# The second mixture-of-experts layer: the order of its products on TensorE, written as a chain in the source

## The chip, the core and the metric

The kernel runs on one core of a Trainium2 chip. The metric is the device time of one execution in microseconds. Times of before are the median of three runs. Engines are named as the profile names them: PE is TensorE's matmul, PEld its weight load, DVE is VectorE, ACT ScalarE, POOL GpSimd, and SP issues the DMAs.

## What is computed

```python
x = attention(q, k, v, p)              # 4 batches, 8 heads, 576 rows -> 2304 x 512
h = x @ w_in                           # first MoE: 512 -> 2048 -> 512
x = (h * clip(h + 3, 0, 6) / 6) @ w_out
P = exp(x @ w_gate - max)              # 2304 x 8, then 8 rounds of row and column norms
out = zeros
for e in range(8):                     # second MoE: 512 -> 1024 -> 512, per expert
    out += P[:, e:e+1] * (maximum(x @ w1[e], 0) @ w2[e])
```

All is float32. A float32 product is made on PE of three products of halves: a high half that is rounded (`fp32r`) and the remainder, so that each 128x128 weight tile costs three matmuls (high by high, high by low, low by high).

## The kernel before

**Tiling.** The 2304 rows are 6 blocks of 384 columns (`TB`). The 8 experts of the second MoE are cut into 32 groups of 256 hidden units. Blocks are taken in three pairs, called passes here. Stage A (to about 440 us) is attention and the first MoE. Stage B (about 440 to 1010 us) is the first pass, blocks 0 and 1, over all 32 groups. Stage C (about 1010 to 2061 us) is the other two passes; in each of them two groups make a unit, so it has 16 units.

**First layer** (`layer1b`, lines 1137 to 1185). For a pair of blocks and one group it makes seven products instead of eight (a Strassen scheme of the Winograd kind): operands `a11, s3, s2, a22, s1, a12, s4` of the blocks against sums of weights in `wa` and `wb`. A product is six matmuls of 384 columns into a PSUM bank (tag `ph`, four banks). Three of the seven add onto a bank that holds an earlier product, so the earlier value must have been read out: `held` copies it (ACT, line 385), `plus` adds it (DVE, line 1165). Four results leave through `finish`: in stage B a Relu on ACT and a split into halves `hs`; in stage C one DVE operation that also multiplies by the share of the expert (line 1128).

**Second layer.** In stage B `layer2b` makes, per group, six products of six matmuls with 512 columns, lines 1463 to 1465, each added into the result by DVE (line 1487). In stage C `layer2s` makes 14 products of six matmuls with 384 columns per unit (lines 1373 to 1375), seven operands by two halves `c`, into four banks of tag `po`; `summed` (DVE, line 1385) adds each into the result. Its operands are made by `h_operands` from the eight results of the unit's two first layers: 14 splits (ACT, line 1321, then a subtraction on POOL or DVE, line 1328) and 8 sums, `mix` (line 1334). `a11` and `s3` can be made after the first of the two first layers, the other five only after the second.

**Weights.** In stage B `combined`, `plain_second` and `keep_second` load, combine and split each group's weights (DVE, POOL and ACT) and store the results in DRAM. Stage C only loads them back (`w` 1024 KB, `w1x` 768 KB, `w2s` 512 KB each) through SP, into two, two and seven buffers.

**What sets the order.** Nothing is issued in the order of the source. `Order.op` records operations with their dependences; `Order.run` builds the order of every engine's queue before the kernel runs: it takes, again and again, the open operation that can start first by the planner's own clock, ties by `prio`. Its clock goes by costs such as `t_pe`, `t_dve`, `t_pool`; `SYNC` (0.2 us) lies between an operation and whoever depends on it. An operation of `alt` may go to POOL or DVE, whichever ends first, with `spare` added to DVE's side; `copy` likewise to ACT or DVE. Each engine then executes its queue in that order. Before the change the products of stages B and C have no order of their own, only operands, banks and `prio`.

## Time and profile before

| | us |
|---|---|
| median of three runs (2077.38 to 2078.06) | 2077.91 |
| the profiled execution, its own time | 2076.28 |
| its span, first to last instruction | 2074.5 |
| PE busy | 1921.8 (93%) |
| DVE busy | 1559.1 (75%) |
| POOL busy | 999.7 (48%) |
| ACT busy | 873.1 (42%) |

Busy shares are means over three stages. A busy PE is not a PE at its peak: its matmuls overlap, so the distance from one start to the next counts, not the duration. The clock column of a window is the share of TensorE's full clock that was granted; 1.00 is 2.4 GHz and 0.5 is 1.2 GHz.

### The profile page before, as it was taken

The page shows a single profiled execution, that of the slowest core. Times are in us where ns is not written, and L with a number is a line of the kernel's source. Part 1 is how long each engine was busy: PE and PEld are TensorE (multiplying, and loading weights), DVE is VectorE, ACT ScalarE, POOL GpSimd, SP SyncE. Part 2 cuts the span into 40 slices and gives each one's busy share as a digit, 9 for nine tenths or more (in the row PEclk, how much of TensorE's full clock was granted, in tenths as well). Part 3 has the DMA queues.
Part 4 walks back from the last instruction along what each step waited for, and adds up shares of the span by engine and source line. Part 5 has one row for each costly group of instructions (what it writes and reads, how often), then busy time and mean ns, then how long its engine had stood idle before and what let it go on. Part 6 is the DMA issues. An engine that isn't in the chain of part 4 may idle for free.

```text
span 2074.5 us, 31172 instructions
## 1 busy us (share of the span) xinstructions
PE 1921.8 (93%) x11199; PEld 1800.5 (87%) x11199; DVE 1559.1 (75%) x2536; ACT 873.1 (42%) x1898; POOL 999.7 (48%) x886
## 2 busy tenths in 40 slices
PE   6999999998899999898999999999989999999997
PEld 4889999897788878887898988989889898988987
DVE  6765674559988887888668778787787878778786
ACT  5764663345455555555432323223243323323232
POOL 3333562357667665667434435344364434334343
PEclk8999999999999999999999999999999999999998
DMA  9931230027788777777777677777777767777762
GB/s 200 198 77 42 62 117 20 3 80 270 269 289 292 277 279 249 279 269 260 265 252 237 228 230 238 235 238 228 230 224 242 239 218 238 232 240 237 220 223 71
DMA packets 189563, 430.22 MB, mean 207 GB/s; under 512 B 52304, under 2 KB 102624, under 8 KB 177120
## 3 DMA queue, kind: packets, MB, share of 16 engines
q1 hardware_dynamic: 189408, 428.23, 64.0%
q8 instruction: 88, 1.44, 0.3%
q14 instruction: 67, 0.55, 0.1%
HBM read 305.94 MB, written 122.23 MB: 206 GB/s over the span
## 4 chain that ended last, share of the span: by engine, by line
PE 57%; DVE 28%; issue 7%; DMA 3%; ACT 3%; POOL 2%; SPq 1%; DVEq 0%; ACTq 0%; POOLq 0%
PE ph L1151 7%; PE ph L1153 7%; PE ph L1152 7%; DVE tmp L1334 7%; PE po L1373 5%; PE po L1374 5%; PE po L1375 5%; DVE tmp L1165 3%; DVE tmp L1128 3%; PE po L1028 3%; PE po L1030 3%; PE po L1029 3%; PE po L1465 2%; PE po L1463 2%; PE po L1464 2%
## 5 line engine op out<-in xcount | busy, mean ns | idle before, releaser
L1328 POOL TENSOR_TENSOR xy<-tmp,xy 128x384 fp32r<-128x384 f32 x191 | 234.3, 1246 | 307.9 <-PE ph L1153 233.1
L1328 POOL TENSOR_TENSOR ax<-tmp,ax 128x384 fp32r<-128x384 f32 x154 | 187.5, 1234 | 282.3 <-PE ph L1153 221.5
L385 ACT ACTIVATE tmp<-ph 128x384 f32<-128x384 f32 x282 | 137.6, 488 | 440.8 <-PE ph L1153 434.9
L503 POOL TENSOR_TENSOR hs<-tmp,hs 128x384 fp32r<-128x384 f32 x193 | 211.0, 1103 | 231.9 <-ACT hs L498 224.7
L1165 DVE TENSOR_TENSOR tmp<-ph,tmp 128x384 f32<-128x384 f32 x288 | 157.4, 552 | 116.2 <-PE ph L1153 100.3
L1334 DVE TENSOR_TENSOR tmp<-tmp,tmp 128x384 f32<-128x384 f32 x253 | 226.7, 914 | 6.3 <-POOL ax L1328 0.5
L1385 DVE TENSOR_TENSOR acc<-po,acc 128x384 f32<-128x384 f32 x304 | 160.8, 552 | 84.8 <-PE po L1375 84.5
L1373 PE MATMUL po<-xy,w2s 128*128 128x384 f32 x492 | 172.8, 351 | 34.0 <-ACT ax L1321 15.3
L1321 ACT ACTIVATE xy<-tmp 128x384 fp32r<-128x384 f32 x246 | 126.8, 524 | 140.6 <-DVE tmp L1334 87.0
L1373 PE MATMUL po<-ax,w2s 128*128 128x384 f32 x404 | 144.0, 356 | 31.7 <-ACT xy L1321 17.2
L1374 PE MATMUL po<-xy,w2s 128*128 128x384 f32 x492 | 170.9, 347 | 0.7 <-DVE xy L1328 0.7
L1375 PE MATMUL po<-xy,w2s 128*128 128x384 f32 x492 | 168.9, 343 | 0.0
L1321 ACT ACTIVATE ax<-tmp 128x384 fp32r<-128x384 f32 x202 | 104.1, 523 | 126.0 <-DVE tmp L1334 71.3
L1151 PE MATMUL ph<-ax,w 128*128 128x384 f32 x448 | 152.9, 341 | 3.5 <-ACT tmp L385 2.0
L1463 PE MATMUL po<-w,hs 128*128 128x512 f32 x384 | 150.8, 393 | 4.0 <-DVE acc L1487 2.7
L1487 DVE SCALAR_TENSOR_TENSOR acc<-po,Pr,acc 128x512 f32<-128x512 f32 x168 | 123.2, 743 | 40.8 <-PE po L1465 40.4
L1153 PE MATMUL ph<-ax,w 128*128 128x384 f32 x448 | 152.4, 340 | 0.0
L1152 PE MATMUL ph<-ax,w 128*128 128x384 f32 x448 | 152.2, 340 | 0.0
L1465 PE MATMUL po<-w,hs 128*128 128x512 f32 x384 | 149.8, 390 | 0.5 <-DVE hs L503 0.5
L1464 PE MATMUL po<-w,hs 128*128 128x512 f32 x384 | 149.7, 390 | 0.0
L1374 PE MATMUL po<-ax,w2s 128*128 128x384 f32 x404 | 142.3, 352 | 0.5 <-POOL ax L1328 0.5
L1128 DVE SCALAR_TENSOR_TENSOR tmp<-tmp,PB 128x384 f32<-128x384 f32 x192 | 133.8, 699 | 10.5 <-DMA PB<-pd 5.5
(230 smaller groups left out, 5579.5 us busy)
## 6 DMA issues: line engine op xcount, KB each, us to landing
w2s<-w2d SPq DMA_DIRECT2D x224, 512.0 KB, 4.3
w<-w1d SPq DMA_DIRECT2D x64, 1024.0 KB, 6.0
w1x<-w1d SPq DMA_DIRECT2D x64, 768.0 KB, 4.7
raw<-in_moe_w_dram SPq DMA_DIRECT2D x64, 512.0 KB, 5.2
w1d<-w SPq DMA_DIRECT2D x32, 1024.0 KB, 5.0
w1d<-w1x SPq DMA_DIRECT2D x32, 768.0 KB, 5.1
w2d<-w SPq DMA_DIRECT2D x96, 256.0 KB, 3.6
w2d<-H SPq DMA_DIRECT2D x64, 256.0 KB, 4.0
```

Source lines behind the costliest of these rows:

```text
L503: lambda e: e.tensor_tensor(dst(w.t[1]), src(), as_f32(dst(w.t[0])), ALU.subtract),
L1128: lambda: nc.vector.scalar_tensor_tensor(c.t, src(), 0.0, pb.t[:, half * TB:(half + 1) * TB], ALU.max, ALU.mult),
L1151: nc.tensor.matmul(out, wh[:, at + c, :], bh[:, c, :], start=first and c == 0, **on)
L1152: nc.tensor.matmul(out, wh[:, at + c, :], bl[:, c, :], start=False, **on)
L1153: nc.tensor.matmul(out, wl[:, at + c, :], bh[:, c, :], start=False, **on)
L1165: t_dve(n), lambda: nc.vector.tensor_tensor(u.t, ps.t[:, :n], u.t, ALU.add),
L1321: t_act(TB), lambda: nc.scalar.activation(dst(0), t.t, AF.Copy),
L1328: lambda e: e.tensor_tensor(dst(1), t.t, as_f32(dst(0)), ALU.subtract),
L1334: t_dve(TB), t_pool(TB), lambda e: e.tensor_tensor(dst.t, i0.t, i1.t, how),
L1373: nc.tensor.matmul(o, wh[:, f, cs], ah[:, f, :], start=begin and f == 0, **on)
L1374: nc.tensor.matmul(o, wh[:, f, cs], al[:, f, :], start=False, **on)
L1375: nc.tensor.matmul(o, wl[:, f, cs], ah[:, f, :], start=False, **on)
```

## The change

`next_pe` puts every product of `layer1b`, `layer2b` and `layer2s` into one chain: each depends on the one before it, with no `SYNC` between them (`tight`). The three functions become generators that stop after each product, and `by_turns` steps through the first layer of the next group, taking one product of the waiting second layer after each of its own. In stage C a unit's two first layers, 14 products, so alternate with the 14 second-layer products of the unit before. At the border of the two passes of stage C seven second-layer products go ahead and seven take turns; after the last unit all 14 go alone.

The planner's costs are set anew for the operations around these products: 0.174 and 0.228 us a matmul, 0.56 us for a DVE operation from PSUM, 0.8 (DVE) and 1.2 (POOL) for one on two SBUF operands; `mix` now goes to DVE only where it ends 0.5 us sooner. `fourth_phase` opens its buffers when the weights are prepared; four `w2s` buffers and three operand buffers open later (`fifth_phase`), when the last second layer of stage B is done; the output of a pass (`written`) is recorded after the first unit's first layers of the next.

```diff
+PITCH, WIDE = 0.174, 0.228
+MIXES = 0.5
+D_PSUM, D_BOTH, D_SHARE, A_PSUM, A_SBUF, P_BOTH = 0.56, 0.8, 0.72, 0.5, 0.53, 1.2
...
-                a.ready = max(a.ready, o.end + SYNC)
+                a.ready = max(a.ready, o.end + (0.0 if a.tight and o.tight else SYNC))
...
         for tag, n, count, first in (("PB", 2 * TB, 2, 0), ("U", 2 * TB, 1, 0), ("tmp", TB, 6, 6)):
             places(tag, fixed(later, tag, n, count, first))
             opened(tag, count)
+
+    def fifth_phase():
+
         wide = [wp.tile([128, 2048], F32R, tag=f"w2_{i}", name=f"w2s{i}") for i in range(2)]
-        places("w2s", [t[:, i:i + 1024] for t in wide for i in (0, 1024)] + [*spot["raw"][:2], (dp, "ms0")])
-        opened("w2s", 7)
+        places("w2s", [t[:, i:i + 1024] for t in wide for i in (0, 1024)])
+        opened("w2s", 4)
         places("xy", spot["hs"])
         opened("xy", 3)
+
+    def raw_over():
+
+        places("w2s", [*spot["raw"][:2], (dp, "ms0")])
+        opened("w2s", 3)
...
+    def next_pe(cost, fn, **kw):
+
+        turns["b"] = [pe(cost, fn, after=turns["b"], tight=True, **kw)]
...
-                t_dve(TB),
+                D_SHARE,
...
-            pe(t_pe(n, 6), mm, reads=[w, src], writes=[ps], after=turns["l1"], **kw)
+            next_pe(6 * PITCH, mm, reads=[w, src], writes=[ps], **kw)
 
         def held(ps):
 
             u = tmp()
-            copy(lambda: u.t, lambda: ps.t[:, :n], n, reads=[ps], writes=[u], **quick)
+            copied(lambda: u.t, lambda: ps.t[:, :n], reads=[ps], writes=[u], **quick)
...
-                t_dve(n), lambda: nc.vector.tensor_tensor(u.t, ps.t[:, :n], u.t, ALU.add),
+                D_PSUM, lambda: nc.vector.tensor_tensor(u.t, ps.t[:, :n], u.t, ALU.add),
...
         b0, b1, b2 = (psum("ph") for _ in range(3))
         product(b0, wa, 0, o["a11"], True)
         p1 = held(b0)
+        yield
         product(b1, wb, 2, o["s3"], True)
         p7 = held(b1)
+        yield
         product(b0, wb, 0, o["s2"])
         u2 = held(b0)
...
         product(b0, wa, 4, o["s4"])
         finish(tmp(), 0, 1, b0)
-        return order.all[-1]
+        yield
...
             high = act(
-                t_act(TB), lambda: nc.scalar.activation(dst(0), t.t, AF.Copy),
+                A_SBUF, lambda: nc.scalar.activation(dst(0), t.t, AF.Copy),
                 reads=[t], fills=[hop[nm]], after=begun[-1:] if c == 0 else [], **quick,
             )
             if c == 0:
                 begun.append(high)
             alt(
-                t_dve(TB), t_pool(TB),
+                D_BOTH, P_BOTH,
...
             alt(
-                t_dve(TB), t_pool(TB), lambda e: e.tensor_tensor(dst.t, i0.t, i1.t, how),
-                reads=reads, writes=[dst], **quick,
+                D_BOTH, P_BOTH, lambda e: e.tensor_tensor(dst.t, i0.t, i1.t, how),
+                reads=reads, writes=[dst], spare=MIXES, **quick,
...
-            pe(t_pe(TB, 3 * NFC), mm, reads=[w, hop[nm]], writes=[ps], **kw)
+            next_pe(6 * PITCH, mm, reads=[w, hop[nm]], writes=[ps], **kw)
...
-            if last and nm == "s2":
-                both(cb, 0)
-                both(cb, 2)
-                both(ca, 2)
+                if last and nm == "s2" and c:
+                    both(cb, 0)
+                    both(cb, 2)
+                    both(ca, 2)
+                yield
...
-            pe(t_pe(512, 3 * NFC), mm, reads=[w2, hs], writes=[ps], **kw)
+            next_pe(3 * NFC * WIDE, mm, reads=[w2, hs], writes=[ps], **kw)
...
+        waiting = iter(())
+
+        def by_turns(one, other):
+
+            for _ in one:
+                next(other, None)
+
+        done, preparing = [], []
...
                 stored[4] = [*wa.writers, *wb.writers]
                 w2, r = plain_second(g, turn)
+                preparing += order.all[at:]
...
-                done.append(layer1b(i, ops[0], wa, wb, rectified(prios(i)[1], hs)))
-                for h in (1, 0):
-                    layer2b(i, g, h, w2, hs[h])
+                by_turns(layer1b(i, ops[0], wa, wb, rectified(prios(i)[1], hs)), waiting)
+                done.append(turns["b"][0])
+                waiting = chain_of(*[layer2b(i, g, h, w2, hs[h]) for h in (1, 0)])
...
+            at = len(order.all)
             keep_second(d2, ws, rs, turn - 0.7)
-        order.op([("", 0.0, fourth_phase)], after=order.all[begun:])
-        late_ops = [o for o in order.all[begun:] if fin[0] in o.holds or fin[1] in o.holds]
+            preparing += order.all[at:]
+        order.op([("", 0.0, fourth_phase)], after=preparing)
+        order.op([("", 0.0, raw_over)], after=preparing)
...
+                if behind and d2 == 0:
+                    for _ in range(NFC * 7 // 2):
+                        next(waiting)
                 for n in range(2):
                     wa, wb = kept_first(G1 + 2 * d2 + n, turn + 0.1 + 0.1 * n)
                     one_of = {}
-                    done.append(layer1b(i, ops[pr], wa, wb, shared(prios(i)[1], pb, one_of)))
+                    by_turns(layer1b(i, ops[pr], wa, wb, shared(prios(i)[1], pb, one_of)), waiting)
...
+                            [("", 0.0, fifth_phase)],
+                            after=[o for o in order.all if any(h.tag in ("w2", "hs") for h in o.holds)],
+                        )
+                        late_ops = [o for o in order.all[begun:] if fin[0] in o.holds or fin[1] in o.holds]
+                        order.op([("", 0.0, more)], after=late_ops)
...
+                if behind and d2 == 0:
+                    written(i, pr - 1, behind)
+                    i += 1
                 w2s = {nm: kept_second(d2, nm, turn + 0.5 + 0.01 * n) for n, nm in enumerate(PLACE)}
                 turn += 1
-                layer2s(i, hop, w2s, C, U, d2 == len(doubles) - 1)
+                waiting = layer2s(i, hop, w2s, C, U, d2 == len(doubles) - 1)
                 i += 1
+            behind = C
             if pr + 1 < NB // 2:
                 ops[pr + 1] = operands(pr + 1, 45, lambda n: [turns["hop"][-1]])
-            written(i, pr, C)
-            i += 1
+        by_turns(waiting, iter(()))
+        written(i, pr, C)
```

Lines of the changed program are 27 to 34 higher: 1178 to 1180 are the first layer's matmuls, 1406 to 1408 and 1497 to 1499 the second layer's, 1361 is the split's subtraction and 1367 `mix`.

PE in stage C, before: the end of the next unit's first first-layer product, and the first product of operand `a12` (here in `xy11`), whose bank is `po_0`, and the start of the next (`c` = 1).

```order
L1153 MATMUL ph_0_13128<-xy7_10112,w10_13013 128x384
L1373 MATMUL po_0_13062<-xy11_13060,w2s1_10688 128x384
L1374 MATMUL po_0_13062<-xy11_13060,w2s1_10688 128x384
L1375 MATMUL po_0_13062<-xy11_13060,w2s1_10688 128x384
L1373 MATMUL po_0_13062<-xy11_13060,w2s1_10688 128x384
L1374 MATMUL po_0_13062<-xy11_13060,w2s1_10688 128x384
L1375 MATMUL po_0_13062<-xy11_13060,w2s1_10688 128x384
L1373 MATMUL po_1_13075<-xy11_13060,w2s1_10688 128x384
```

And with the change, the same operand's first product (here from `ax1`) in a unit of the same pass:

```order
L1180 MATMUL ph_3_13365<-ax0_112,w10_13225 128x384
L1406 MATMUL po_2_13377<-ax1_113,w2s2_13210 128x384
L1407 MATMUL po_2_13377<-ax1_113,w2s2_13210 128x384
L1408 MATMUL po_2_13377<-ax1_113,w2s2_13210 128x384
L1406 MATMUL po_2_13377<-ax1_113,w2s2_13210 128x384
L1407 MATMUL po_2_13377<-ax1_113,w2s2_13210 128x384
L1408 MATMUL po_2_13377<-ax1_113,w2s2_13210 128x384
L1178 MATMUL ph_2_13474<-ax0_112,w10_13225 128x384
```

Before, this product follows one product of the next unit and is followed by the rest of its own second layer; now it follows five products of the next unit and has one more on either side of it.

PE in stage B, before: a first-layer product into `ph_2`, one other product, and the next product onto `ph_2`.

```order
L1153 MATMUL ph_2_7806<-ax1_113,w11_7700 128x384
L1151 MATMUL ph_3_7947<-ax1_113,w11_7700 128x384
L1152 MATMUL ph_3_7947<-ax1_113,w11_7700 128x384
L1153 MATMUL ph_3_7947<-ax1_113,w11_7700 128x384
L1151 MATMUL ph_3_7947<-ax1_113,w11_7700 128x384
L1152 MATMUL ph_3_7947<-ax1_113,w11_7700 128x384
L1153 MATMUL ph_3_7947<-ax1_113,w11_7700 128x384
L1151 MATMUL ph_2_7806<-xy6_5333,w11_7700 128x384
```

And with the change, around a product of `layer2b` (1497 to 1499), where the bank `ph_1` of the last row was last written two products before the one that ends in the first row:

```order
L1180 MATMUL ph_2_7931<-ax1_113,w11_7673 128x384
L1497 MATMUL po_1_7943<-w20_7643,hs2_7814 128x512
L1498 MATMUL po_1_7943<-w20_7643,hs2_7814 128x512
L1499 MATMUL po_1_7943<-w20_7643,hs2_7814 128x512
L1497 MATMUL po_1_7943<-w20_7643,hs2_7814 128x512
L1498 MATMUL po_1_7943<-w20_7643,hs2_7814 128x512
L1499 MATMUL po_1_7943<-w20_7643,hs2_7814 128x512
L1178 MATMUL ph_1_7821<-xy6_5363,w11_7673 128x384
```

Two products of one bank had one first-layer product between them; now they have one first-layer and two second-layer products.

POOL in stage C, before, at the end of a unit's first layers: subtractions of splits only.

```order
L1328 TENSOR_TENSOR xy11_13060<-tmp9_13001,xy11_13060 128x384
L1328 TENSOR_TENSOR xy12_13072<-tmp10_13040,xy12_13072 128x384
L1328 TENSOR_TENSOR xy13_13084<-tmp7_12965,xy13_13084 128x384
L1328 TENSOR_TENSOR xy12_13072<-tmp6_13028,xy12_13072 128x384
L1328 TENSOR_TENSOR xy13_13084<-tmp0_12957,xy13_13084 128x384
L1328 TENSOR_TENSOR xy14_13097<-tmp3_12857,xy14_13097 128x384
L1328 TENSOR_TENSOR xy15_13111<-tmp9_13001,xy15_13111 128x384
```

And with the change, at the same place:

```order
L1367 TENSOR_TENSOR tmp10_12865<-tmp10_12865,tmp11_12999 128x384
L1367 TENSOR_TENSOR tmp5_12816<-tmp10_12865,tmp5_12816 128x384
L1361 TENSOR_TENSOR xy6_13047<-tmp3_12983,xy6_13047 128x384
L1367 TENSOR_TENSOR tmp6_12938<-tmp7_12841,tmp6_12938 128x384
L1361 TENSOR_TENSOR xy11_13064<-tmp7_12841,xy11_13064 128x384
L1361 TENSOR_TENSOR ax1_113<-tmp8_12964,ax1_113 128x384
L1361 TENSOR_TENSOR ax1_113<-tmp9_13077,ax1_113 128x384
```

Sums (`mix`, 1367) now stand among the subtractions. Over the whole program `mix` stands 127 times on POOL and 129 times on DVE, where it was 3 and 253; the subtractions of these splits are 319 on POOL and 129 on DVE, where they were 345 and 103. The number of matmuls and of DMAs is the same.

## Rows read from the trace of the kernel before

**Rows 1.** The page: busy time, share of the span and instructions of each engine.
```profile
PE 1921.8 (93%) x11199; PEld 1800.5 (87%) x11199; DVE 1559.1 (75%) x2536; ACT 873.1 (42%) x1898; POOL 999.7 (48%) x886
```

**Rows 2.** Windows of two stretches: busy us and instructions per engine, clock, DMA share.
```profile
core 0: us, PE busy (x) PEld busy (x) DVE busy (x) ACT busy (x) POOL busy (x), PEclk, DMA share, GB/s
600.00:1000.00 400.00, 370.15 (x1812) 330.19 (x1811) 330.25 (x427) 212.15 (x453) 259.26 (x224) 0.98 0.76 267
1100.00:2000.00 900.00, 840.03 (x4646) 818.41 (x4645) 697.94 (x1079) 277.31 (x572) 374.52 (x309) 0.98 0.72 232
```

**Rows 3.** PE timeline: start, duration, line, operation; 384 columns, then 512 columns.
```profile
1499.73 0.34 PE L1153 MATMUL ph<-xy,w1x 128*128 128x384 f32 x1
...
1511.17 0.34 PE L1153 MATMUL ph<-ax,w 128*128 128x384 f32 x1
...
705.39 0.39 PE L1463 MATMUL po<-w,hs 128*128 128x512 f32 x1
...
713.33 0.39 PE L1465 MATMUL po<-w,hs 128*128 128x512 f32 x1
```

**Rows 4.** Waits of PE, 1100 to 2000 us: total us, times, longest.
```profile
PE po L1373 <- ACT xy L1321: 25.2, 14, 2.0
PE po L1373 <- ACT ax L1321: 23.0, 12, 2.8
PE po L1373 <- DVE acc L1385: 8.3, 17, 1.2
```

**Rows 5.** PE timeline at one such wait, and the window behind it.
```profile
1162.52 0.41 PE L1373 MATMUL po<-ax,w2s 128*128 128x384 f32 x1 [1.78 <-ACT xy L1321]
...
1164.30 0.53 PE L1374 MATMUL po<-ax,w2s 128*128 128x384 f32 x1
1164.62 0.53 PE L1375 MATMUL po<-ax,w2s 128*128 128x384 f32 x1
...
1163.40:1166.80 3.40, 3.40 (x12) 3.33 (x12) 3.40 (x7) 0.53 (x1) 1.71 (x2) 0.51 0.08 29
```

**Rows 6.** DVE groups, 1100 to 2000 us: busy us, mean ns, idle before.
```profile
L1334 DVE TENSOR_TENSOR tmp<-tmp,tmp 128x384 f32<-128x384 f32 x216 | 193.4, 914 | 5.7 <-POOL ax L1328 0.5
L1385 DVE TENSOR_TENSOR acc<-po,acc 128x384 f32<-128x384 f32 x272 | 143.8, 552 | 71.9 <-PE po L1375 71.6
L1128 DVE SCALAR_TENSOR_TENSOR tmp<-tmp,PB 128x384 f32<-128x384 f32 x164 | 114.3, 697 | 4.6
L1328 DVE TENSOR_TENSOR xy<-tmp,xy 128x384 fp32r<-128x384 f32 x44 | 46.0, 1046 | 0.0
```

**Rows 7.** POOL and ACT groups of the same stretch.
```profile
L1328 POOL TENSOR_TENSOR xy<-tmp,xy 128x384 fp32r<-128x384 f32 x164 | 200.9, 1244 | 267.2 <-PE ph L1153 214.2 <-ACT xy L1321 53.0
...
L1321 ACT ACTIVATE xy<-tmp 128x384 fp32r<-128x384 f32 x208 | 107.6, 524 | 119.8 <-DVE tmp L1334 73.5 <-DVE tmp L1128 46.3
L385 ACT ACTIVATE tmp<-ph 128x384 f32<-128x384 f32 x164 | 80.2, 489 | 378.2 <-PE ph L1153 376.0
```

**Rows 8.** Single lines, whole span: shortest/median/longest ns, first and last start.
```profile
L1334 DVE TENSOR_TENSOR tmp<-tmp,tmp x253: 543/902/1386, 1022.5 to 2050.2; 128x384 f32<-128x384 f32 x127
...
L1328 POOL TENSOR_TENSOR xy<-tmp,xy x191: 997/1325/1357, 1030.2 to 2047.2; 128x384 fp32r<-128x384 f32 x191
...
L1165 DVE TENSOR_TENSOR tmp<-ph,tmp x288: 506/551/559, 452.7 to 2040.4; 128x384 f32<-128x384 f32 x144
```

**Rows 9.** Groups of PE and DVE, 600 to 1000 us, and the waits of PE.
```profile
L1463 PE MATMUL po<-w,hs 128*128 128x512 f32 x276 | 108.0, 391 | 2.7 <-DVE acc L1487 2.7
...
L1487 DVE SCALAR_TENSOR_TENSOR acc<-po,Pr,acc 128x512 f32<-128x512 f32 x139 | 102.0, 744 | 34.3 <-PE po L1465 34.1
...
PE ph L1151 <- DVE tmp L1165: 26.7, 16, 3.6
```

**Rows 10.** Two lines of 430 to 1010 us: shortest/median/longest ns.
```profile
L1248 DVE TENSOR_TENSOR T<-T,H x37: 675/1221/1812, 462.0 to 977.9; 128x512 fp32r<-128x512 f32 x37
...
L503 POOL TENSOR_TENSOR hs<-tmp,hs x193: 1000/1022/1550, 59.6 to 1002.3; 128x384 fp32r<-128x384 f32 x193
```

32 lines of the change are left out of this document (25 added, 7 removed).

## The prediction

> **What bounds the kernel now.** I read the page's first section first: PE is busy 93% of the span, DVE 75%, POOL 48% and ACT 42% [rows 1]. So the end is PE's, and the question is how far each stage of it is from PE's own pace. That pace I took from the timeline of undisturbed stretches: 67 matmuls of 384 columns start from 1499.73 to 1511.17, 66 steps of 173.3 ns; 36 matmuls of 512 columns from 705.39 to 713.33, 35 steps of 226.9 ns [rows 3]. The floor of a stage B group is then 42 x 0.1733 + 36 x 0.2269 = 15.45 us, that of a stage C unit 168 x 0.1733 = 29.12 us.
>
> Then the windows, to see how far the stages are from it. Stage B, 600 to 1000 us: line 1463 ran 276 times, 12 a group, so 23.0 groups in 400 us, **17.39 us a group** [rows 2, 9]. Stage C, 1100 to 2000: 4646 matmuls, 24 of them the output's transposes (six times four, by the source), so 4622 / 168 = 27.5 units in 900 us, **32.7 us a unit** [rows 2]. The distances are 1.94 and 3.6 us.
>
> What they consist of: PE idle is 900 - 840.0 = 60.0 us in C, 2.2 a unit, and 400 - 370.2 = 29.8 us in B, 1.3 a group [rows 2]. The waits say on whom. In C it is line 1373, the second layer's first matmul, that waits: 25.2 + 23.0 us for ACT's split of an operand (1321) and 8.3 us for DVE's sum (1385), 56.5 of the 60.0 us [rows 4]. In B it is the first layer waiting for DVE's read of a bank (1165), 26.7 of 29.8 us [rows 9]. The rest, 1.4 us a unit and 0.6 a group, is PE running slower or starting again: after a wait of 1.78 us the matmuls start 0.32 us apart for 3.4 us at a granted clock of 0.51, the lower of the two levels [rows 5]. Such stretches come back through C (mean clock 0.98 [rows 2]).
>
> **The change part by part.**
>
> Stage C, the operands' wait. Five of seven operands can only be made when both first layers are done. Before, one product of the next unit and four of the second layer stood between that point and the first product of `a12`: 5 x 1.04 = 5.2 us of cover, and PE waited about 2 us behind them. Now five products of the next unit and four of the second layer stand there (the order's first two pieces): 9.4 us, 4.2 us more than before, against waits of at most 2.8 us [rows 4]. Later operands gain more: up to twelve more first-layer products lie ahead of `s4`. So this term, 48.2 / 27.5 = 1.75 us a unit, goes. What is late next is not an operand but a bank: DVE's sum of 0.55 us [rows 6] must be done before the bank is written again, four products later before (4.2 us) and four pairs later now (8.3 us). Those 8.3 / 27.5 = 0.3 us go as well, unless DVE itself runs behind.
>
> Does it? DVE is busy 697.9 / 27.5 = 25.4 us a unit [rows 2]. By the order 124 `mix` leave it and 26 subtractions come, over 32 units: -124 x 0.914 + 26 x 1.05 = -86 us [rows 6], 2.7 a unit, so 22.7 us. At the floor of 29.12 that is 78%, as now (25.4 of 32.7). POOL is busy 13.6 us a unit and takes 124 more at 1.24 and loses 26: +122 us, 3.8 a unit, so 17.4 us, 60% [rows 2, 7]. ACT keeps 10.1 us. None of them reaches PE's floor.
>
> That DVE needs longer when POOL is busy is in the rows: 1334 takes 543 ns at the shortest, 902 in the median and 1386 at the longest, POOL's 1328 997 and 1325, while 1165, with one operand in PSUM, stays at 506 to 559 [rows 8]. With POOL at 60% instead of 42% the 14 DVE operations of a unit that read two SBUF operands (4 `mix`, 4 subtractions, 6 of 1128) lie between no change and 1.39 us each. They are in the 22.7 at 0.91, 1.05 and 0.70 [rows 6]; at 1.39 it would be 1.9 + 1.4 + 4.2 = 7.5 us more, 30.2 us. I take a third of that, 25 us (86%), nearest to the medians.
>
> The Trainium skill (SBUF — State Buffer, "Who interferes with whom") says of this that a VectorE instruction with two SBUF inputs and a GpSimd instruction that reads SBUF hold one port pair in turn, each for its whole length. The trace agrees in what it shows (543 to 1386 ns against 506 to 559). By that rule moving sums from the engine that holds the pair for 0.55 us to one that holds it for 1.0 us speaks against this change; its result is the third case below.
>
> So PE should be fed in C, but with DVE at 86% and every engine's queue in a fixed order I leave something: one wait of a sum per unit as now (8.3 / 17 = 0.49 us [rows 4]) and 0.4 us of lower clock, 0.9 in all. A unit goes from 32.7 to 30.0, a gain of 2.7 us, **86 us over 32 units**. Bounds: half of the idle and nothing of the clock (1.1 us, 35) to all but 0.4 us (3.2 us, 102).
>
> Loads in C: the DMA share is 0.72 [rows 2]; the same bytes in 30.0 us make 0.78. Stage B runs at 0.76 and 267 GB/s, more than the 232 x 32.7 / 30.0 = 253 GB/s needed. The loads are issued when a product frees a buffer, now evenly over the unit instead of in bursts. I cost them at nothing. The operand and weight buffers that open later hold nothing up: the first second layer of C starts a unit later than they did.
>
> Stage B. The bank that waits for 1165 had one first-layer product as cover, 1.04 us; now one first-layer and two second-layer products, 1.04 + 2 x 1.36 = 3.8 us (the order's next two pieces). By cover alone the 1.16 us a group would go. But DVE is busy 330.3 / 23.0 = 14.4 us a group [rows 2], 93% of the floor, and no DVE work leaves stage B to speak of. Of that, 1487 (102.0 us) and 1165 (69 x 0.551 = 38) read PSUM, 6.1 us; 8.3 us read two SBUF operands and are stretched: 1248 has a median of 1221 ns against 675 at the shortest [rows 9, 10]. At the shortest lengths these are 8.3 x 675 / 1221 = 4.6 us, and POOL's 259.3 / 23.0 = 11.3 us are 11.3 x 1000 / 1022 = 11.1 [rows 2, 10]; if one always waits for the other, as the stretch suggests, that is 15.7 us, more than PE's floor. So DVE and POOL become the bound soon after PE's waits are gone. I take 16.8 us a group (DVE at 86%, the two together at 93%), a gain of 0.6, half of the waits, over 28 of 32 groups since the first four run beside the routing: **17 us**. Bounds: 0 to 1.6 us, 45 in all.
>
> Edges. The last unit's 14 second-layer products have no partner in either program; at the border of the passes seven go ahead alone and seven first-layer products go alone later, much as before. Zero, within 5 us either way. The chain itself adds a wait only in the planner; PE's queue is in order before and after. But a late product now also holds up the other layer's product behind it, which the planner used to let past; that is the fifth case.
>
> Sum: 86 + 17 = 103 us. The profiled execution took 2076.28 (span 2074.5 and 1.8 around it), 1.6 under the median of three. The span would be 1971.5, the median **1975 us**.
>
> **The rivals.**
> 1. As above, 1975. For it: PE's waits are nearly all of the two kinds that get more cover. Against it: DVE's stretch.
> 2. Stage B gains nothing: the 15.7 us of DVE and POOL in turn, with the gaps that two queues in fixed order leave, are its 17.39 us now. 2078 - 86 = 1992. For it: DVE's stretch there; against it: PE's waits for 1165 have a cover that is too short by 1 to 3 us, which is what changes.
> 3. Stage C is paced by DVE stretched to its limit: 30.2 us of work at 97% fill makes 31.1 us a unit, a gain of 1.6 x 32 = 51; with B's 17, 2010; without, 2027.
> 4. Everything goes: C at 29.5 a unit and B at 15.8: 102 + 45 = 147, so 1931.
> 5. Slower. ACT's queue is in order: the copies of `held` (0.49 us [rows 7]) stand between splits (1321) that wait for `mix`, now half of them on POOL at 1.24 us. The bank is needed again 3.1 us after its product. If the four `mix` of a unit on POOL each come so late that a copy behind them misses that by 1.24 us, PE stands 5.0 us a unit, and no product of the other layer may pass: 29.12 + 5.0 + 1.4 (the clock as now) = 35.5 us, +2.8 x 32 = 90; with 17 from B, 2151. It decides from 3.6 us of waits a unit, 0.26 us per pair. Against it: planned 1.2 us for POOL is what the rows show, and 3.1 us of cover hides two such operations in a row.
>
> That the change doesn't do what it says is excluded by the order: the products alternate one by one in all of stages B and C.
>
> **How the numbers follow.** Chances: the first 0.52, the second 0.19, the third 0.13, the fourth 0.09, the fifth 0.05, and 0.02 for an end within 0.2%, which is what a measurement here can tell from no change (4 us). Faster by more 0.93, slower by more 0.05. The range takes in the fourth case's end and the third's: 1931 to 2027.
>
> **What would show it.** In the changed profile: no wait of a second-layer product for ACT's split in steady units, units of about 30 us between equal products of stage C, the granted clock at 1.00 in more of its slices; POOL near 58 to 60% there; `mix` and split subtractions on DVE longer than 0.91 and 1.05 us; stage B at 16.8 us a group with PE still waiting for DVE. Case 2 shows as a stage B of unchanged length with DVE above 90%; case 3 as DVE above 95% in C and PE waiting for 1385; case 5 as first-layer products waiting for ACT's copies. The forecast is wrong if PE's idle time in C stays above 1.5 us a unit, or if a load's landing ends PE's waits.

## The result: 1982 us, and the profile after

The changed kernel took **1982.03 us** in the median (1980.3 to 1984.49, four runs), the kernel before 2077.98 beside it. The ratio is 0.9536, 95% interval 0.9519 to 0.9552: faster by 4.6%. The forecast was 1975 us. The sum is right within 7 us, its parts are not: stage C gave 12.6 us more than forecast, stage B 12 less, and 8 us that were not forecast went at the end of stage A. That these nearly cancel is luck.

Both programs run the same 11199 matmuls, and both traces hold them all, so that an equal number left marks an equal point in the work. I cut both where 7600 are left (the routing is over) and where 5200 are left (early in stage C). Windows of before, then of after; the columns are start and end of the window, its length, busy us and instructions of each engine, PE's granted clock, DMA share and GB/s:

```profile
0.00:526.10 526.10, 489.79 (x3598) 443.09 (x3599) 344.20 (x756) 285.00 (x666) 240.53 (x245) 0.98 0.40 109
526.10:1052.80 526.70, 488.47 (x2401) 438.64 (x2400) 427.01 (x568) 273.65 (x584) 331.46 (x289) 0.98 0.78 272
1052.80:2074.50 1021.70, 943.56 (x5203) 918.81 (x5201) 787.87 (x1214) 314.44 (x649) 427.71 (x353) 0.97 0.70 225
```

```profile
0.00:534.30 534.30, 494.01 (x3598) 444.85 (x3599) 343.40 (x756) 287.86 (x669) 242.89 (x249) 0.97 0.39 107
534.30:1056.00 521.70, 488.41 (x2402) 439.28 (x2401) 435.15 (x557) 278.07 (x591) 334.86 (x294) 0.98 0.79 276
1056.00:1979.10 923.10, 904.51 (x5203) 900.14 (x5201) 738.92 (x1122) 302.21 (x642) 510.82 (x444) 1.00 0.72 248
```

Stage C gave 98.6 us, stage B 5.0, and the stretch ahead of it cost 8.2. The sum, 95.4, is the difference of the spans. Stage B's 5.0 us are no more than two traces of one order differ by, as e8 shows below.

Inside the stages, after (they answer to [rows 2]; in 600 to 1000 us the 1840 matmuls, 78 a group, make 16.96 us a group):

```profile
600.00:1000.00 400.00, 376.21 (x1840) 335.63 (x1839) 341.29 (x428) 218.92 (x466) 266.12 (x236) 0.98 0.80 280
1100.00:1400.00 300.00, 300.00 (x1729) 300.00 (x1728) 242.18 (x371) 96.77 (x205) 165.68 (x144) 1.00 0.75 260
```

In C, 1729 / 168 = 10.29 units in 300 us are **29.15 us a unit**, against a floor of 29.12. DVE is busy 23.5 us of it (81%), POOL 16.1 (55%). PE's waits from 1050 to 1900 us are few, and all lie at the border of the two passes, where before the same list was one wait or two in each unit [rows 4]:

```profile
PE po L1406 <- ACT acc L402: 2.7, 1, 2.7
PE ph L1179 <- DVE xy L1100: 1.6, 2, 1.4
PE ph L1178 <- ACT tmp L412: 1.4, 1, 1.4
```

Earlier, in the first unit of stage C (1000 to 1050 us), PE waits once for a load of weights from DRAM; before, the same stretch had 3.5 us of waits, for DVE and POOL:

```profile
PE ph L1178 <- DMA w<-w1d: 4.5, 1, 4.5
```

The groups of DVE and POOL in C (1100 to 1900 us, answering to [rows 6, 7]) show the stretch that the forecast feared: `mix` on DVE went from 914 to 1057 ns, the product with the share (`L1155`) from 697 to 800, while operations with one operand in PSUM stayed at 550. The splits' subtractions on DVE did not lengthen (1046 before, 1038 after). PE didn't wait for any of them.

```profile
L1418 DVE TENSOR_TENSOR acc<-po,acc 128x384 f32<-128x384 f32 x261 | 143.5, 550 | 87.3 <-PE po L1408 87.2
L1155 DVE SCALAR_TENSOR_TENSOR tmp<-tmp,PB 128x384 f32<-128x384 f32 x161 | 128.6, 800 | 4.5
L1367 DVE TENSOR_TENSOR tmp<-tmp,tmp 128x384 f32<-128x384 f32 x109 | 113.2, 1057 | 0.9
L1367 POOL TENSOR_TENSOR tmp<-tmp,tmp 128x384 f32<-128x384 f32 x107 | 110.3, 1031 | 293.1 <-DVE tmp L1155 291.0
L1361 DVE TENSOR_TENSOR xy<-tmp,xy 128x384 fp32r<-128x384 f32 x74 | 75.9, 1038 | 1.3
```

Stage B keeps its kind of wait (600 to 950 us, answering to the last line of [rows 9]); the first line is of before, the second of after:

```profile
PE ph L1151 <- DVE tmp L1165: 23.1, 15, 3.1
PE ph L1178 <- DVE tmp L1192: 19.2, 11, 2.5
```

And what the forecast didn't have: at the end of stage A, PE's timeline shows first-layer products of stage B from 394.6 us on, where they had begun at 439.1, and gaps around them. Here are three of the rows, then two windows of after, then the same two of before:

```profile
394.55 0.45 PE L1178 MATMUL ph<-ax,w 128*128 128x384 f32 x1 [0.36 <-DVE tmp L1035]
...
397.12 0.44 PE L1178 MATMUL ph<-ax,w1x 128*128 128x384 f32 x1 [1.26 <-DVE tmp L1035]
...
410.41 1.40 PE L1557 MATMUL ph<-acc,wg 128*32 128x384 f32 x5 [2.54 <-DVE pwl L979]
```

```profile
400.00:425.00 25.00, 22.11 (x155) 19.55 (x154) 7.76 (x16) 6.01 (x13) 5.32 (x6) 0.93 0.00 1
425.00:450.00 25.00, 23.18 (x145) 20.65 (x143) 9.36 (x18) 10.76 (x24) 9.00 (x10) 1.00 0.08 32
```

```profile
400.00:425.00 25.00, 25.00 (x168) 23.36 (x167) 9.67 (x20) 6.07 (x12) 4.38 (x6) 1.00 0.01 1
425.00:450.00 25.00, 25.00 (x149) 24.08 (x148) 12.28 (x20) 9.10 (x20) 9.37 (x9) 1.00 0.00 1
```

The old code put a first-layer product behind `turns["l1"]`, the last first-layer product of stage A; `next_pe` dropped that dependence, so that the planner let stage B's first products in between stage A's last ones.

### The profile page after: what moved, and what is told of

Read it like the earlier page. It is cut to its first block, busy times and chain, and to the rows that moved or that the text cites. A ratio compares the mean times of both kernels' runs of the same rounds, so it can differ in the third digit from the quotient of the medians.

```text
span 1979.1 us, 30944 instructions
## 1 busy us (share of the span) xinstructions
PE 1886.9 (95%) x11199; PEld 1784.3 (90%) x11199; DVE 1517.5 (77%) x2434; ACT 868.1 (44%) x1901; POOL 1088.6 (55%) x985
## 4 chain that ended last, share of the span: by engine, by line
PE 71%; DVE 12%; DMA 6%; POOL 4%; issue 3%; ACT 3%; SPq 1%; POOLq 0%; DVEq 0%; ACTq 0%
PE ph L1178 9%; PE ph L1180 9%; PE ph L1179 9%; PE po L1408 8%; PE po L1407 8%; PE po L1406 8%; PE po L1055 3%; PE po L1057 3%; PE po L1056 3%; DMA raw<-in_moe_w_dram 2%; PE ph L1017 2%; PE po L1499 2%; PE po L1497 2%; PE po L1498 1%; PE ph L1019 1%
## 5 line engine op out<-in xcount | busy, mean ns | idle before, releaser
L1367 POOL TENSOR_TENSOR tmp<-tmp,tmp 128x384 f32<-128x384 f32 x127 | 131.2, 1033 | 347.3 <-DVE tmp L1155 344.9
L1354 ACT ACTIVATE xy<-tmp 128x384 fp32r<-128x384 f32 x296 | 147.2, 519 | 344.1 <-DVE tmp L1155 299.6
L1361 POOL TENSOR_TENSOR xy<-tmp,xy 128x384 fp32r<-128x384 f32 x209 | 252.8, 1223 | 45.4 <-ACT xy L1354 44.3
L1406 PE MATMUL po<-xy,w2s 128*128 128x384 f32 x592 | 198.9, 336 | 1.3 <-DVE U L1418 1.3
L1408 PE MATMUL po<-xy,w2s 128*128 128x384 f32 x592 | 199.6, 337 | 0.0
L1407 PE MATMUL po<-xy,w2s 128*128 128x384 f32 x592 | 199.6, 337 | 0.0
L1178 PE MATMUL ph<-ax,w 128*128 128x384 f32 x512 | 174.0, 340 | 3.2 <-ACT tmp L412 2.0
L1179 PE MATMUL ph<-ax,w 128*128 128x384 f32 x512 | 173.4, 339 | 0.6 <-POOL ax L1100 0.6
L1180 PE MATMUL ph<-ax,w 128*128 128x384 f32 x512 | 173.5, 339 | 0.0
L1155 DVE SCALAR_TENSOR_TENSOR tmp<-tmp,PB 128x384 f32<-128x384 f32 x192 | 153.3, 799 | 5.3
L1361 POOL TENSOR_TENSOR ax<-tmp,ax 128x384 fp32r<-128x384 f32 x110 | 134.6, 1236 | 21.2 <-ACT ax L1354 20.6
L1354 ACT ACTIVATE ax<-tmp 128x384 fp32r<-128x384 f32 x152 | 76.7, 519 | 144.3 <-DVE tmp L1155 118.9
L1367 DVE TENSOR_TENSOR tmp<-tmp,tmp 128x384 f32<-128x384 f32 x129 | 132.1, 1042 | 1.1
L525 ACT ACTIVATE hs<-tmp 128x384 fp32r<-128x384 f32 x224 | 117.2, 523 | 23.4 <-DVE tmp L1035 11.8
```

The costliest lines, as they stand in the source:

```text
L1178: nc.tensor.matmul(out, wh[:, at + c, :], bh[:, c, :], start=first and c == 0, **on)
L1179: nc.tensor.matmul(out, wh[:, at + c, :], bl[:, c, :], start=False, **on)
L1180: nc.tensor.matmul(out, wl[:, at + c, :], bh[:, c, :], start=False, **on)
L1354: A_SBUF, lambda: nc.scalar.activation(dst(0), t.t, AF.Copy),
L1361: lambda e: e.tensor_tensor(dst(1), t.t, as_f32(dst(0)), ALU.subtract),
L1367: D_BOTH, P_BOTH, lambda e: e.tensor_tensor(dst.t, i0.t, i1.t, how),
```

## The experiments

Each kernel's trace holds the 11199 matmuls and is cut in the same way, in us: from the first instruction to the matmul with 7600 left (A), from there to the one with 5200 left (B), and on to the start of the last matmul (C). B ends with some 200 matmuls of stage C. Each ratio is to executions of the kernel before that ran beside that kernel. The cuts are of one execution each: the beginning of A, down to 10500 matmuls left, took 95.9 to 100.9 us in five kernels with one order of PE there (changed, e1, e2, e3, e12).

| kernel | median | ratio (95%) | A | B | C |
|---|---|---|---|---|---|
| before | 2077.98 | 1 | 526.3 | 526.7 | 1012.0 |
| changed | 1982.03 | 0.9536 (0.9519 to 0.9552) | 534.6 | 521.6 | 913.6 |
| e1 chain from stage A | 1974.53 | 0.9502 (0.9476 to 0.9528) | 529.0 | 521.6 | 913.6 |
| e2 stage B in blocks | 2016.22 | 0.9690 (0.9656 to 0.9723) | 539.0 | 554.5 | 913.6 |
| e12 blocks turned | 1988.05 | 0.9554 (0.9541 to 0.9567) | 529.9 | 534.3 | 913.6 |
| e3 stage C in sevens | 1992.22 | 0.9589 (0.9555 to 0.9623) | 533.1 | 526.7 | 917.8 |
| e5 chain, old elementwise costs | 1987.5 | 0.9579 (0.9563 to 0.9596) | 534.2 | 525.3 | 916.0 |
| e4 all costs, no chain | 2012.2 | 0.9679 (0.9650 to 0.9708) | 525.0 | 527.8 | 949.3 |
| e10 elementwise costs, no chain | 1994.85 | 0.9610 (0.9578 to 0.9642) | 521.4 | 524.9 | 928.8 |
| e9 matmul costs, no chain | 2153.32 | 1.0368 (1.0339 to 1.0397) | 530.7 | 514.6 | 1097.2 |
| e8 spare for `mix`, no chain | 2076.85 | 1.0006 (0.9994 to 1.0018) | 528.4 | 521.4 | 1013.0 |
| e6 no low halves of sums in B | 1961.86 | 0.9455 (0.9437 to 0.9473) | 531.5 | 506.6 | 913.5 |
| e7 preparation on POOL | 1971.36 | 0.9490 (0.9472 to 0.9508) | 525.4 | 521.7 | 913.7 |
| e11 chain in C only | 1967.98 | 0.9478 (0.9461 to 0.9496) | 527.5 | 511.5 | 913.5 |

### The end of stage A (e1)

```diff
+        turns["b"] = turns["l1"]
 
         def by_turns(one, other):
```

> The changed kernel with one line more: the chain begins behind stage A's last first-layer product, the dependence that every first-layer product of the second MoE had before. Theory: the changed kernel lost 9 us ahead of stage B because two of its products, with their operands and copies, went into stage A's tail (the last second-layer product of stage A starts at 459.5 us instead of 450.2, the routing's first matmul at 467.8 instead of 456.2). Then stage A's last product comes back to 450 to 452 us, and the total falls by 7 to 11 us, from 1982 to 1971 to 1975. Rival: the time before stage B is hidden by DVE's routing chain and the weights of stage B, which set its pace anyway; then stage A ends earlier but the total stays within 2 us of 1982.

The chain begins behind stage A's last first-layer product, and the stretch A falls from 534.6 to 529.0 us, the median by 7.5. PE is busy again in the two windows that had gaps:

```profile
400.00:425.00 25.00, 25.00 (x170) 23.36 (x169) 9.14 (x21) 6.91 (x14) 5.01 (x5) 1.00 0.01 1
425.00:450.00 25.00, 24.71 (x145) 23.48 (x144) 11.85 (x18) 9.00 (x20) 8.50 (x8) 1.00 0.00 1
```

So 5.6 of the 8.3 us lost ahead of stage B come from the dropped dependence. Where stage A ends, between 8600 and 7800 matmuls left, the three kernels are clearer apart: 129.6 us before, 137.9 with the change, 130.7 in e1. B and C don't move, and the expected 7 to 11 us came (the two intervals just overlap).

### Stage C: the chain or the costs (e3, e4, e5, e8, e9, e10)

Is it the one-by-one order? e3 keeps the chain and lets seven products of each layer alternate:

```diff
-                    by_turns(layer1b(...), waiting)
+                    by_turns(layer1b(...), iter(()))
+                    for _ in range(NFC * 7 // 2):
+                        next(waiting, None)
```

> The changed kernel, but in stage C seven first-layer products alternate with seven second-layer products of the unit before, not one with one; chain, look-ahead and costs stay. Theory one (stage C's gain is the cover of the operands, which a look-ahead of a unit gives in any grain): waits for ACT's split stay away, a unit takes 29.1 to 29.5 us, total 1982 to 1995. Theory two (the fine grain itself is needed, since banks and the two engines' queues get bursts): a unit takes 30.5 us or more, total 2025 or above.

C takes 4.2 us more, 29.35 us a unit, so the grain matters little; what counts is that other products stand between the end of a unit's first layers and the second-layer product that would wait (how many is counted below). (Another 5.1 us lie ahead of the cut: PE's order is the changed kernel's down to 5455 matmuls left, and the loss comes behind that point, where stage C begins, 58.5 instead of 53.8 us to 5200 left.)

e4 takes the costs of the change and no chain: the kernel before with `PITCH`, `WIDE`, `MIXES`, `D_*`, `A_*` and `P_BOTH` in the same places.

> The kernel before with the planner's new costs alone: the costs of these products, of DVE from PSUM, of DVE and POOL on two SBUF operands, and the 0.5 us for sums; no chain, no turns. Theory one (the order does it): stage C stays near 32 us a unit with waits for ACT's split, total 2060 to 2085. Theory two (true costs and sums on POOL do it): stage C falls to 29.1 to 30 us a unit, total 1980 to 2005.

Neither theory had this: 62.7 of stage C's 98.4 us come with the planner's costs alone. The window and the waits of e4:

```profile
1100.00:1400.00 300.00, 292.11 (x1669) 288.99 (x1668) 250.16 (x371) 90.04 (x190) 161.94 (x134) 1.00 0.76 250
```

```profile
PE po L1386 <- DVE U L1398: 18.8, 13, 4.1
PE po L1386 <- DVE acc L1398: 5.9, 7, 0.9
```

30.2 us a unit, and the wait that is left is for DVE's sum of a bank, not for a split. e5 asks the reverse, the chain with the old elementwise costs, which send `mix` back to DVE:

```diff
-MIXES = 0.5
-D_PSUM, D_BOTH, D_SHARE, A_PSUM, A_SBUF, P_BOTH = 0.56, 0.8, 0.72, 0.5, 0.53, 1.2
+MIXES = 0.0
+D_PSUM, D_BOTH, D_SHARE, A_PSUM, A_SBUF, P_BOTH = 0.465, 0.465, 0.465, 0.37, 0.415, 0.976
```

> The changed kernel with its chain of products, but with the elementwise costs of before in the planner (0.465 us for each DVE operation of 384 columns, 0.37 and 0.415 for ACT, 0.976 for POOL, nothing added to DVE's side for mix): mix goes back to DVE (254 of 256). Theory one, the chain gives the operands their cover whatever the planner believes of the other engines: stage C keeps 29.2 to 29.6 us a unit, and the time is 1980 to 1995 us. Theory two, the chain fixes only PE's order and the balance of DVE and POOL needs the new costs: DVE at 25 us a unit runs behind, stage C goes to 30 us a unit or more, and the time is 2005 us or more.

Its window of stage C, and the group of `mix` on DVE (1100 to 1900 us):

```profile
1100.00:1400.00 300.00, 300.00 (x1728) 300.00 (x1728) 240.38 (x405) 97.60 (x205) 135.49 (x112) 1.00 0.75 258
```

```profile
L1367 DVE TENSOR_TENSOR tmp<-tmp,tmp 128x384 f32<-128x384 f32 x214 | 174.7, 816 | 1.0
```

C is 2.4 us longer than with the new costs, at 29.17 us in steady units, with POOL busy 135 us of 300 instead of 166 and DVE nearly the same: with the chain, the elementwise costs and the balance of DVE and POOL hardly count. (e5 keeps the new matmul costs and the change's other edits, when buffers open and where the output is recorded; these were not taken out one by one.) e8, the kernel before with `spare=0.5` on `mix`, was to test that balance without a chain.

> The kernel before with one number changed: mix goes to DVE only where it ends 0.5 us sooner than on POOL. No chain, and all other costs of the planner as before. Theory one, the part of the gain that came with the costs alone (2012 us) comes from the balance of DVE and POOL in stage C: the time falls to 2045 us or less. Theory two, it comes from the order of the products that the planner chooses with truer durations, and that order is nearly the old one here: 2060 to 2085 us.

It tests less than it should: with DVE's old cost of 0.465 us the margin moves one `mix` (252 on DVE, 253 before). Time and C are those of before. But it shows how far two traces of one order differ: up to 1000 us, all of stage B but its end, every engine runs the same operations in the same order as before, and B took 521.4 us against 526.7. So a gain of 5 us in B is not shown by one trace. e9 and e10 cut the costs of e4 in two: e9 has this edit and those of the two second layers' matmuls (`PITCH`, `WIDE`), e10 the others (`D_*`, `A_*`, `P_BOTH`, `MIXES`).

```diff
-            pe(t_pe(n, 6), mm, reads=[w, src], writes=[ps], after=turns["l1"], **kw)
+            pe(6 * PITCH, mm, reads=[w, src], writes=[ps], after=turns["l1"], **kw)
```

> The kernel before with only the planner's costs of the elementwise operations set anew (DVE 0.56, 0.72 and 0.8 us, ACT 0.5 and 0.53, POOL 1.2, and 0.5 us on DVE's side for mix), no chain, matmul costs as before; mix goes to POOL 95 times of 256 instead of 3, and second-layer products come between first-layer ones more often (runs of 1 to 4, as with all costs). Theory one, the gain of the run with all new costs came from the matmul costs: 2060 us or more, stage C 32 us a unit or more. Theory two, it came from the elementwise costs, because a planner that sees the operands come later puts first-layer products in front of the product that would wait: stage C 31 us a unit or less and 2035 us or less.

> The kernel before with only the planner's costs of a matmul set anew (0.174 and 0.228 us instead of 0.163 and 0.216), no chain and all elementwise costs as before; mix stays on DVE (254 of 256). In the run with all new costs and no chain (2012 us) stage C took 30.3 us a unit and its products alternated more. Theory one, that gain came from the matmul costs, by which the planner's PE order follows the real one: stage C 31 us a unit or less and 2035 us or less. Theory two, it came from the elementwise costs: stage C 32 us a unit or more, 2060 to 2085 us.

e10 went as its theory two says (29.5 us a unit in 1100 to 1400 us), e9 came out slower than either theory allowed. The halves pull in opposite directions: the elementwise costs alone bring 83.2 of the 98.4 us, the matmul costs alone, 0.011 to 0.012 us more for each, lose 85.2. The order of PE's products of one unit (1 a first layer, 2 the second layer), from the traces in steady units; e10 has two kinds of unit in turn. In the rows of before, e9 and e10 the first run of 1 and the next single 1 are still this unit's own first layers, and only later ones the next unit's; in the last two rows all are the next unit's:

```
before   111111111111 22 1 22 1 2222222222
e9       111111111111 2 1 222 1 2222222222
e10      111111111 222 1 2 11111 2222222222
         11111111 2 1 222 11 2 11 222222222
changed  1212121212121212121212121212
e3       1111111 2222222 1111111 2222222
```

A planner that sees the elementwise operations end later keeps three or four more first-layer products for the place where PE would wait, as the chain does everywhere. e9's order on PE differs from that of before by one product, and its units took 300 x 168 / 1453 = 34.7 us. So the trace must say what PE waits for. PE at one unit of e9 (start, duration), then DVE and ACT at that time:

```profile
1512.88 0.34 PE L1154 MATMUL ph<-xy,w 128*128 128x384 f32 x1
1516.53 0.66 PE L1374 MATMUL po<-ax,w2s 128*128 128x384 f32 x1 [3.31 <-ACT tmp L386]
```

```profile
1512.88 1.81 DVE L1335 TENSOR_TENSOR tmp<-tmp,tmp 128x384 f32<-128x384 f32 x2
1514.61 1.34 DVE L1329 TENSOR_TENSOR ax<-tmp,ax 128x384 fp32r<-128x384 f32 x1
1515.88 0.55 DVE L1386 TENSOR_TENSOR U<-po,U 128x384 f32<-128x384 f32 x1
...
1515.15 0.47 ACT L386 ACTIVATE tmp<-ph 128x384 f32<-128x384 f32 x1
```

The row names ACT's copy, which ended at 1515.62, 0.9 us before PE started. DVE's sum ended at 1516.43, 0.10 us before, and does so at 21 of the 22 waits of over 1.5 us at this line from 1100 to 1900 us. The product is the first of operand `a12`: it adds onto the bank that `a11`'s product filled, and so waits for the sum that reads that bank, besides its operand. The sum stands in DVE's queue behind two `mix` and a subtraction. In the kernel before the same product waits for both too:

```profile
1128.67 1.19 DVE L1334 TENSOR_TENSOR tmp<-tmp,tmp 128x384 f32<-128x384 f32 x1
1129.78 0.55 DVE L1385 TENSOR_TENSOR U<-po,U 128x384 f32<-128x384 f32 x1
...
1129.89 0.52 ACT L1321 ACTIVATE xy<-tmp 128x384 fp32r<-128x384 f32 x1 [0.59 <-DVE tmp L1334]
...
1130.43 0.41 PE L1373 MATMUL po<-xy,w2s 128*128 128x384 f32 x1 [1.75 <-ACT xy L1321]
```

The sum ends 0.10 us ahead of PE there, the split 0.01 us. But this split is not one of `a12`: ACT stood idle ahead of it until the `mix` that ends at 1129.86, so it splits that result, while `a12` is split from a first-layer result as it stands, without a `mix`. A row names the operation that ended last on an engine that the product waits for, whether the product needs that operation or not. At all 26 waits of [rows 4] that name a split it is so: the split follows a `mix` by 0.03 or 0.04 us and ends 0.01 us before PE, and the sum of `a11`'s bank, behind that same `mix` in DVE's queue, ends 0.10 us before. So the 48.2 us are waits for the sum, in the kernel before as in e9 and, mostly one product later, in e4. What removes them is room ahead of the product. Between a unit's last first-layer product and its first product of `a12` stand 3 products before (PE waits 1.8 us), 4 in e9 (3.3 us, behind the longer queue above), 5 or 6 in e4 and e10, 10 with the change and 18 in e3; from 5 on PE no longer waits at this product in steady units. Between the two products of the bank stand 5 before and only 3 in e3, so what counts is the time that DVE has for the `mix` ahead of the sum, not the distance within the bank.

### Stage B (e2, e6, e7, e11, e12)

e2 keeps the chain and makes stage B's order blocks of seven first-layer and six second-layer products:

```diff
-                by_turns(layer1b(...), waiting)
+                by_turns(layer1b(...), iter(()))
...
+                by_turns(waiting, iter(()))
```

> The changed kernel, but in stage B the seven first-layer products of the next group stand together and then the six second-layer products of this one; the chain, the look-ahead of one group and the costs stay. Theory one (stage B is paced by DVE and POOL): the turns are worth little there, 0 to 0.3 us a group, total 1982 to 1992. Theory two (the cover of a bank by 3.8 instead of 1.04 us is what stage B gains): waits for DVE's read of the bank come back to 1.1 us a group, 17.2 to 17.4 us a group, total 1994 to 2002.

Its window of stage B, and PE's waits there:

```profile
600.00:1000.00 400.00, 365.22 (x1712) 323.27 (x1711) 315.65 (x405) 209.95 (x443) 245.32 (x217) 0.94 0.74 262
```

```profile
PE ph L1178 <- DVE tmp L1192: 20.6, 14, 3.7
PE ph L1178 <- ACT tmp L412: 9.5, 6, 1.9
```

B grows by 33 us, more than either theory gave it: taking turns is worth that much against these blocks in this chain. Besides the waits (600 to 950 us) the granted clock falls to 0.94.

e6 takes DVE's work away: it leaves out the low halves of the four combined second-layer weight tiles.

```diff
-            alt(
-                t_dve(512), t_pool(512),
-                lambda e, t=t, h=h: e.tensor_tensor(t.t.bitcast(F32R), t.t, as_f32(h.t), ALU.subtract),
-                reads=[h], writes=[t], prio=prio, spare=SPARE,
-            )
...
-                (2, k), 256, kept_at(nm, 1).rearrange("p (c n) -> p c n", c=NFC), lambda t=t: t.t, [t], prio
+                (2, k), 256, kept_at(nm, 1).rearrange("p (c n) -> p c n", c=NFC), lambda h=h: h.t, [h], prio
```

> The changed kernel, leaving out in stage B the subtractions that make the low halves of the four combined second-layer weight tiles (64 operations of 512 columns on DVE or POOL; the high half is stored in the low half's place, so loads and stores stay the same). Theory one, DVE's backlog with the weight preparation makes stage B's waits of 16.82 against a floor of 15.45 us a group: with two operations of some 0.9 to 1.6 us less in each group the group falls to 16.2 us or less, and the time by 15 us or more, to 1967 us or less. Theory two, the rest of a group above its floor is something else (weight loads, the clock, PE itself): the group stays within 0.2 us and the time within 6 us of 1982.

The same window and waits of e6:

```profile
600.00:1000.00 400.00, 382.52 (x1890) 341.28 (x1889) 297.44 (x409) 224.20 (x477) 249.33 (x224) 0.99 0.82 291
```

```profile
PE ph L1178 <- ACT tmp L412: 14.8, 7, 3.6
```

B loses 15 us and the median 20, as theory one says, but the group goes only from 16.96 to 16.51 us in this window, not to the 16.2 expected. DVE is busy 297 us of 400 instead of 341, POOL 249 instead of 266, DVE's wait is gone, and PE now waits for ACT's copies (they end 0.05 us ahead of PE, DVE's and POOL's operations 0.3 us or more). So this load holds 0.45 of the 1.51 us that a group takes above its floor, and ACT is next.

e7 moves that load to POOL: e1, with the planner's DVE cost of the weight preparation raised.

```diff
+def t_both(n):
+    return 0.45 + n / 900.0
...
-                t_dve(512), t_pool(512),
+                t_both(512), t_pool(512),
...
```

> The changed kernel with the chain carried on from stage A's products (as in the first experiment, 1974.5 us), and the planner's DVE cost of stage B's weight preparation raised from the bare duration to one near the stretched durations of the trace (0.45 us + 1 us for each 900 columns), so that more of it goes to POOL: of the 32 sums of 1024 columns 28, of the splits 142 of 176. Theory one, DVE's backlog in stage B comes from an under-estimated cost: the group falls from 16.87 to 16.0 to 16.4 us and the time to 1955 to 1968 us. Theory two, work taken to POOL comes back as longer durations of both engines, or as weights that are ready later: the group stays at 16.7 us or more and the time at 1970 us or more.

Its window of stage B, and the group of POOL's largest operations (600 to 950 us):

```profile
600.00:1000.00 400.00, 377.58 (x1840) 332.44 (x1839) 318.85 (x382) 222.64 (x469) 333.82 (x278) 0.99 0.79 279
```

```profile
L534 POOL TENSOR_TENSOR w<-raw,w 128x1024 fp32r<-128x1024 f32 x19 | 47.5, 2502 | 0.0
```

Theory two for stage B, 521.7 us as in e1. The median is 3 us under e1's, with intervals that overlap. Against the changed kernel's window DVE loses 22 us of its 341, POOL gains 68: an operation of 1024 columns takes 2502 ns on POOL, and 1274 on DVE in the changed kernel. The Trainium skill (Perfetto Trace Analysis, "Optimizing Scalar/DVE Operations") says that, since GpSimd and VectorE share an SBUF read port, offloading between those two might not help; this run agrees (521.7 us with the offloading, 521.6 without).

The parts suggest a better version: the chain where it gives, and stage B by the planner, with the costs under which e9's B took 514.6 us. e11 is the changed kernel with the flag `free` set for stage B: its products leave the chain, its first-layer products stand behind `turns["l1"]` again, and `held` and `plus` also go by `copy` and `t_dve` again:

```diff
-        turns["b"] = [pe(cost, fn, after=turns["b"], tight=True, **kw)]
+        if turns["free"]:
+            turns["free"] = pe(cost, fn, after=turns["l1"] if kw.pop("first", False) else [], **kw)
+        else:
+            kw.pop("first", None)
+            turns["b"] = [pe(cost, fn, after=turns["b"], tight=True, **kw)]
...
```

> The changed kernel with the chain in stage C only. Stage B's products go by operands, banks and prio again, as before, with the elementwise costs of before for the operations on their banks and the new matmul costs; PE's order there is that of the run with matmul costs alone (seven and six products in blocks, 16.59 us a group, stage B's last product at 999.6 us), and stage A's tail is that of before. Theory one, the parts add: stage B ends near 1000 us, stage C keeps 29.2 us a unit, and the time is 1960 to 1968 us. Theory two, the group of 16.6 us in that run came from something that these edits do not carry over (the order of DVE, ACT and POOL with all old elementwise costs): the group stays at 16.8 us or more and the time at 1972 us or more.

Its windows of stages B and C:

```profile
600.00:1000.00 400.00, 380.86 (x1896) 339.64 (x1895) 317.27 (x430) 209.62 (x457) 276.03 (x258) 1.00 0.81 281
1100.00:1400.00 300.00, 300.00 (x1728) 300.00 (x1727) 243.69 (x369) 98.82 (x210) 169.14 (x147) 1.00 0.75 261
```

The parts add: **1967.98 us**, 14 under the changed kernel and the lowest median here of a kernel that computes the whole result (its interval overlaps those of e1 and e7; its B is 10 us under theirs). Its stage B has blocks of seven and six as e2's has, but cut elsewhere: the six second-layer products stand after the first two of a group, as cover for the two copies that the third and fourth wait for. (Four of a group's seven products, the third, fourth, fifth and seventh, add onto a filled bank, not three.) e12, which has e1's line too, puts e2's blocks at that place in the chain:

```diff
-                by_turns(layer1b(i, ops[0], wa, wb, rectified(prios(i)[1], hs)), waiting)
+                first = layer1b(i, ops[0], wa, wb, rectified(prios(i)[1], hs))
+                for _ in range(2):
+                    next(first)
+                by_turns(waiting, iter(()))
+                by_turns(first, iter(()))
```

> The changed kernel with the chain carried on from stage A's products, all its new costs, and another order in the chain of stage B alone: two first-layer products of a group, then the six second-layer products of the group before in one block, then the group's other five. With the blocks of seven and six of an earlier run (the cut between two groups' first layers) stage B took 554 us for the 2400 matmuls between 7600 and 5200 left, the changed kernel 521.6, and the planner's own order without a chain, which has its blocks at the place tried here, 511.5. Theory one, the place of the block decides: the two copies that the first products wait for get the whole block as cover, so stage B takes 508 to 516 us and the time is 1962 to 1970 us. Theory two, the planner's stage B was short because of the order of the other engines (its elementwise costs of before), and a block is as bad here as there: stage B 530 us or more, and the time 1983 us or more.

Its window of stage B:

```profile
600.00:1000.00 400.00, 368.11 (x1798) 326.54 (x1797) 301.39 (x403) 201.74 (x439) 285.15 (x272) 0.99 0.80 274
```

Theory two's figures came (534.3 and 1988.05 us), though not its reason that a block is as bad here as there: 20.2 of the 43 us between e2 and e11 go with the place of the block, 22.8 stay. PE's blocks are then alike, so these lie in the order that the planner makes for the other engines. e4 and e9 say the same: from the fifth group on their PE order in B is one, and B takes 527.8 and 514.6 us. Which operation it is was not found.

## Why the prediction came out

**Stage C: right remedy, term too small.** The forecast was 86 us (32.7 to 30.0 a unit), measured are 98.4. The mis-sized term is the 0.9 us a unit left for "one wait of a sum per unit" and "0.4 us of lower clock": steady units have 0.03. DVE did stretch, and at 23.5 us a unit came within the 22.7 to 25 allowed, but a queue at 81% made no PE wait. POOL was below its forecast (16.1 for 17.4 us), in part because `mix` took 1.03 us there where 1.24 was taken. Behind the cut some 14 us above the floor are left in C, 9.4 of them waits at the border of the passes and at the end.

**The operand's cover: the wrong wait.** That waits go because other products come in between is shown by e3 and e5. But the step put 48.2 us to operands that come too late, by the name in the row (ACT's split), and costed DVE's sum as a small term of its own, 0.3 us a unit. At those waits it is the sum that PE stands on, behind a `mix` in DVE's queue, in [rows 4] as in e9. The cover was miscounted as well: two of the "four of the second layer" come ahead of the unit's last first-layer product, so that 3 products cover the wait before and 10 now, not 5 and 9. Both slips left the outcome as it was, since the same products of the next unit that cover an operand give DVE its time.

**Where the gain comes from was not seen.** The forecast took the costs as a detail that moves `mix`. Without a chain they shorten C by 62.7 us; their halves shorten it by 83 and lengthen it by 85. With the chain the elementwise half is worth 2.4 us there; the old matmul costs were not tried with it.

**Stage B: forecast 17 us, measured 5, which is not clear of what two traces differ by.** From the start of the fifth group to that of the last, 27 groups, a group took 17.38 us before, 17.23 in e8, which has the order of before there, and 17.15 with the change. So the base of 17.39 was right, and the mis-sized term is the gain of 0.6 us, "half of the waits": it came to 0.23, and to 0.08 against e8. From 600 to 950 us the wait for DVE's read of a bank fell from 23.1 to 19.2 us. The reason given, DVE and POOL at their limit behind PE's waits, is borne out in part: less work for them took 0.45 us off a group (e6), work moved between them nothing (e7). But the same work in another order ran at 400 x 78 / 1896 = 16.46 us a group (e11), under the 16.8 that the forecast took for the bound; their order counts, and not only their load.

**Edges: the step that failed.** "Zero, within 5 us either way" was 8.2 us of loss. It looked at the two ends of stage C and not at the place where the chain begins; the line that drops `after=turns["l1"]` stands in the diff. e1 gives back 5.6 of it. "I cost them at nothing", said of the loads, holds in steady units, where PE waits for none; at the beginning of C one load held PE for 4.5 us.

**The rivals.** The second (B gains nothing) is nearly what B did, but C made up for it. The third's condition, DVE above 95%, did not occur. The fifth's price, 35.5 us a unit and 2151 us, is met by e9 (34.7 and 2153) by chance, since e9 has no chain: not through copies behind splits but through a sum behind `mix` on DVE.
